# Inverting the triangular blocks of the last two chunks separately instead of as a pair

## The chip, the cores and the metric

The kernel runs on one core of a Trainium2 chip. The metric is the device time of one execution in microseconds (us); lower is better. A core has engines that run side by side, each with its own queue of instructions taken strictly in order: PE (TensorE: matrix products; PEld is its weight load), DVE (VectorE), ACT (ScalarE), POOL (GpSimd) and SP (SyncE, which here only issues transfers). An instruction whose inputs are not there holds up everything behind it on its own engine.

## The reference

Two parts follow each other: a linear recurrence over time ("attention"), and a mixture of experts.

```python
for t in range(S):                      # S = 768 steps, 4 batches x 8 heads, D = 40
    y[:, :, t] = einsum('bhd,bhde->bhe', r_t, state)
    Sa = einsum('bhde,bhe->bhd', state, a_t)
    state = state * w_t[:, :, None, :] - Sa (x) b_t + v_t (x) k_t
...
P = exp(x @ w_gate - max)               # x = y as 3072 tokens x 320
for _ in range(8):
    P /= P.sum(1) + 1e-9; P /= P.sum(0) + 1e-9; P *= N / E
out = sum over 8 experts of P[:, e:e+1] * (relu(x @ w1[e]) @ w2[e])
```

## The kernel before

The 768 time steps are cut into 12 **chunks** of 64, and the recurrence is rewritten so that within a chunk everything is a matrix product, except that a unit triangular 64x64 matrix has to be inverted for each chunk, batch and head. One chunk of one batch (four pairs of heads) is a **step**, written (chunk, batch). The order of the work comes from a table of events, each with a due time: `prep` (L112) reads the inputs of a step, forms products with running decays, and writes the triangular matrix to a scratch tensor `ld` in DRAM; `recur` (L262) runs the recurrence of a step in five stages, PE and DVE in turn: av (PE) - f (DVE L279) - xc (PE) - pu (PE L297) - pm (DVE L299) - c (PE) - ws (DVE L306) - y, z - zt (PE), then the same batch of the next chunk. Four batches are in flight, one stage apart. A scheduler then fixes each engine's instruction order from the table and its own cost model.

**The inversion** stands between prep and recurrence. The list `GROUPS` says which chunks are inverted together; `GRP` gives each chunk its group and place. A chunk has 4 batches x 8 heads = 32 matrices, each cut into two 32x32 diagonal blocks, so it fills 64 partitions, and a pair of chunks fills 128. One inversion of a group is: `load_lu` (L363) loads the blocks from DRAM into the tile `lu`; `flip_l` (L192, L193), `inv_diag` (L176, L179), `flip_d` (L196), `contract` (L185, L188), `flip_h` (L199) compute the inverse in the tiles `un` and `tn` with DVE instructions alone; `finish` (L358, L360, L361) makes a transposed copy and writes `un` and `tn` to the DRAM tensors `ud` and `nd`. There is one set of tiles `lu`, `un`, `tn`, `pr`, `gt` for all groups. `tload` (L225) loads a chunk's part of them back into the tiles `td`, `lg` and `tt`, and `tmat` (L246) makes the missing off-diagonal block with products gp (L253) and op (L258), twice per chunk, for batches 0-1 and 2-3. The products pu of the chunk (L297) need the result.

The due time of a group's inversion follows its last prep; that of the preps follows the number of the group's first chunk (`t0`).

**The expert part** starts while the recurrence ends: `prep_w` (L497) loads raw weights `ws` (L500) and splits them with ACT and POOL, `prep_x` (L530) reloads the tokens (`xs`, L535 and L537) and splits them with DVE (lines L544 to L560, three units of 128 columns for each of the four parts `s` of the tokens), and then PE runs 128 blocks of products p (L572) and op (L637). Its staging tiles lie where the tiles of prep and inversion lay, so the first load of `ws` comes behind the last inversion.

Of the kernel before, what the change touches and what calls it, by code (L numbers as in the profile page):

```python
# [28 lines left out]
def attention(ctx, tc, d, xd, ps, pq, pt, gs, lg):  # L29
# [355 lines left out]
    for c in range(NCH):  # L385
# [5 lines left out]
        for half in range(2):  # L391
            ev.append((t + 2 * SKEW * half, tmat, (c, half)))
    for s, cs in enumerate(GROUPS):
        us = slice(0, 64 * len(cs))
# [17 lines left out]
            pass  # L412


GROUPS = [[0, 1], [2, 3], [4, 5], [6, 7], [8, 9], [10, 11]]
GRP = {c: (i, j) for i, g in enumerate(GROUPS) for j, c in enumerate(g)}
P0 = -8
PD = 0.75
# [418 lines left out]
```

## Time and profile before

| | us |
|---|---|
| median of 3 runs | 1893.79 (1890.14 to 1895.72) |
| the profiled execution | 1882.69 |
| its span | 1880.9 |
| PE busy in the span | 1774.0 (94%) |
| DVE busy in the span | 1365.8 (73%) |
| the recurrence's last pm (L299) starts at | 548.2 |

The page cuts the span into 40 slices of 47 us; its first 12 slices are the recurrence, the rest are the experts. Rows of a group show the time busy and the mean of one instruction, then the idle time of the engine ahead of it with what ended that. The clock rows (PEclk) give the share of full clock that PE was granted: in this trace it is 1 or 0.5 at any moment, so a window's 0.74 is a mixture. A step (c, b) is known by counting pm, L299: there are 48 of them. PE durations overlap each other, so time is read from starts, or from windows.

### The profile page before, as it was taken

How to read it: one execution, taken by the hardware profiler on the slowest of the kernel's cores; microseconds unless marked ns; L12 is line 12 of the kernel's file. 1: busy time of each engine (PE TensorE's matmuls, PEld its weight loads, DVE VectorE, ACT ScalarE, POOL GpSimd, SP SyncE). 2: the span in 40 equal slices, each digit the busy share in tenths (PEclk: the TensorE clock that was granted, in tenths of full speed). 3: DMA queues.
4: the chain of work that ended last, by engine and by line, in shares of the span. 5: the costliest groups of instructions: out<-in, count | busy, mean ns of one | idle time of the engine just before them, and what ended most of it. 6: DMA issues, size and time to landing. Idle time of an engine off the chain costs nothing.

```text
span 1880.9 us, 31865 instructions
## 1 busy us (share of the span) xinstructions
PE 1774.0 (94%) x12035; PEld 1733.0 (92%) x12035; DVE 1365.8 (73%) x2378; ACT 854.6 (45%) x1845; POOL 867.8 (46%) x846
## 2 busy tenths in 40 slices
PE   4489998899898999999999999999999999999999
PEld 4378887899788899999999999999999999999999
DVE  7865867848558867776777767886776867777676
ACT  6356667466543434343443434445343433434342
POOL 6545546331444345281744628004471826537170
PEclk8579989789689999999999999999999999999999
DMA  7578776685621111020111102111110201111011
GB/s 192 114 152 175 149 174 158 120 140 109 168 67 46 37 37 55 20 74 18 57 37 37 56 19 74 55 33 37 37 55 19 73 19 55 37 37 59 16 37 43
DMA packets 187839, 136.27 MB, mean 72 GB/s; under 512 B 155941, under 2 KB 165285, under 8 KB 187685
## 3 DMA queue, kind: packets, MB, share of 16 engines
q1 hardware_dynamic: 184485, 128.98, 27.7%
q10 hardware_dynamic: 3200, 5.25, 1.1%
q8 instruction: 95, 1.56, 0.4%
q14 instruction: 59, 0.48, 0.1%
HBM read 113.74 MB, written 20.45 MB: 71 GB/s over the span
## 4 chain that ended last, share of the span: by engine, by line
PE 78%; DVE 7%; DMA 7%; POOL 3%; issue 2%; ACT 2%; SPq 1%; ACTq 0%; POOLq 0%; DVEq 0%
PE op L637 35%; PE p L572 32%; DMA inp<-in_inp_dram 3%; PE xc L286 2%; PE pu L297 1%; PE ll L151 1%; PE av L278 1%; PE c L304 1%; PE lp L334 1%; DMA nd<-tn 1%; PE gp L253 1%; DVE pr L185 1%; DMA rb<-in_r_dram 1%; PE op L258 1%; POOL ab L146 1%
## 5 line engine op out<-in xcount | busy, mean ns | idle before, releaser
L572 PE MATMUL p<-xch,wh 128*128 128x384 f32 (+1 forms) x1792 | 605.6, 339 | 6.9 <-DVE u L590 2.4
L593 ACT ACTIVATE hh<-sm 128x384 fp32r<-128x384 f32 x512 | 269.4, 526 | 722.9 <-DVE sm L590 722.9
L637 PE MATMUL op<-wh,hh 128*128 128x320 f32 x1536 | 477.8, 312 | 2.9 <-ACT hh L593 2.8
L637 PE MATMUL op<-wl,hh 128*128 128x320 f32 x1536 | 475.6, 310 | 0.0
L637 PE MATMUL op<-wh,hl 128*128 128x320 f32 x1536 | 468.8, 311 | 2.4 <-DVE hl L596 2.4
L518 POOL TENSOR_TENSOR wl<-ws,wh 128x640 fp32r<-128x640 f32 x60 | 103.3, 1721 | 608.7 <-ACT wh L516 608.5
L596 DVE SCALAR_TENSOR_TENSOR hl<-sm,hh 128x384 fp32r<-128x384 f32 x512 | 368.0, 752 | 2.2 <-ACT hh L593 2.0
L572 PEld LDWEIGHTS p<-xch,wh 128*128 128x128 f32 (+1 forms) x1792 | 337.8, 189 | 10.4 <-DVE u L590 4.1
L572 PE MATMUL p<-xcl,wh 128*128 128x384 f32 x896 | 302.9, 338 | 0.0
L572 PE MATMUL p<-xch,wl 128*128 128x384 f32 x896 | 302.3, 337 | 0.0
L637 PEld LDWEIGHTS op<-wh,hh 128*128 128x128 f32 x1536 | 291.1, 189 | 3.7 <-ACT hh L593 3.7
L637 PEld LDWEIGHTS op<-wl,hh 128*128 128x128 f32 x1536 | 291.6, 190 | 0.0
L637 PEld LDWEIGHTS op<-wh,hl 128*128 128x128 f32 x1536 | 287.6, 188 | 3.2 <-DVE hl L596 3.1
L590 DVE TENSOR_TENSOR sm<-p,u 128x384 f32<-128x384 f32 x384 | 234.8, 621 | 8.8
L572 PEld LDWEIGHTS p<-xcl,wh 128*128 128x128 f32 x896 | 168.9, 188 | 0.0
L572 PEld LDWEIGHTS p<-xch,wl 128*128 128x128 f32 x896 | 168.8, 188 | 0.0
L590 DVE TENSOR_TENSOR sm<-p,p 128x384 f32<-128x384 f32 x128 | 71.3, 557 | 129.7 <-PE p L572 76.9
L590 DVE TENSOR_TENSOR p<-p,p 128x384 f32<-128x384 f32 x128 | 71.2, 556 | 103.6 <-PE p L572 101.6
L590 DVE TENSOR_TENSOR u<-p,p 128x384 f32<-128x384 f32 x128 | 70.8, 553 | 59.8 <-PE p L572 58.7
L526 POOL TENSOR_TENSOR wl<-ss,wh 128x512 fp32r<-128x512 f32 x60 | 90.8, 1514 | 35.3 <-ACT wh L523 31.2
L151 PE MATMUL ll<-ab,kb 104*128 104x128 f32 x336 | 63.7, 349 | 45.9 <-POOL ab L146 21.8
L151 PEld LDWEIGHTS ll<-ab,kb 104*128 104x128 f32 x336 | 55.5, 250 | 50.7 <-POOL ab L146 30.2
(166 smaller groups left out, 2793.9 us busy)
## 6 DMA issues: line engine op xcount, KB each, us to landing
ws<-in_wts_dram SPq DMA_DIRECT2D x60, 832.0 KB
inp<-in_inp_dram SPq DMA_DIRECT2D x42, 521.6 KB
rb<-in_r_dram SPq DMA_DIRECT2D x48, 208.0 KB
ld<-lt ACTq DMA_DIRECT2D x40, 128.0 KB
vz<-in_v_dram SPq DMA_DIRECT2D x48, 104.0 KB
f<-in_vt_dram SPq DMA_DIRECT2D x48, 80.0 KB
xd<-y SPq DMA_DIRECT2D x96, 40.0 KB
st<-in_inp_dram SPq DMA_DIRECT2D x6, 521.6 KB
```

Source lines behind the costliest of these rows:

```text
L146: eng.tensor_tensor(out=ab[64:104, :, 64:128], in0=a_in[64:104], in1=g[64:104], op=ALU.mult)
L151: nc.tensor.matmul(ll[:, p], lhsT=kb[:, p], rhs=ab[:, p], start=True, stop=True)
L185: nc.vector.tensor_tensor(out=prv, in0=a.unsqueeze(2).broadcast_to([nu, n_c, n_r, n_k]), in1=m.unsqueeze(1).broadcast_to([nu, n_c, n_r, n_ ...
L253: nc.tensor.matmul(gp[:, p], lhsT=lb[:, p], rhs=t1[:, p], start=True, stop=True)
L286: nc.tensor.matmul(xc[h][:, p], lhsT=pp["sx"][:, p, h], rhs=f[:, p, h], start=True, stop=True)
L518: g.tensor_tensor(out=wl[:, 0:640], in0=raw[:, 256:896], in1=wh[:, 0:640], op=ALU.subtract)
L526: g.tensor_tensor(out=lv[:, 3:7], in0=so[:, :, 0], in1=hv[:, 3:7, 0], op=ALU.subtract)
L572: nc.tensor.matmul(o, lhsT=w_, rhs=x_, start=(j == 0), stop=(j == 3))
L590: eng.tensor_tensor(out=out, in0=x, in1=y, op=ALU.add)
L593: nc.scalar.activation(out=hh[:, f, h], in_=sm[f][:, h], func=AF.Relu)
L596: v.scalar_tensor_tensor(out=hl[:, f, h], in0=sm[f][:, h], scalar=0.0, in1=hh[:, f, h], op0=ALU.max, op1=ALU.subtract)
L637: nc.tensor.matmul(ops[i], lhsT=a[:, h, cs], rhs=w_[:, cw], start=(f == 0 and h == 0 and j == 0), stop=(last and h == 1 and j == 2))
```

## The change

The pair [10, 11] becomes two groups. Nothing else in the text changes; each of the two groups now has its own scratch tensors, loads, inversion, and write-back.

```diff
-GROUPS = [[0, 1], [2, 3], [4, 5], [6, 7], [8, 9], [10, 11]]
+GROUPS = [[0, 1], [2, 3], [4, 5], [6, 7], [8, 9], [10], [11]]
 GRP = {c: (i, j) for i, g in enumerate(GROUPS) for j, c in enumerate(g)}
```

What it does to the table of events: the inversion of chunk 10 is due right behind the four preps of chunk 10, and that of chunk 11 behind those of chunk 11, where both were due behind all eight. The first prep of chunk 11 is due 0.69 of a time unit later (five units are a chunk), the other seven as before. Two inversions of 64 partitions stand where one of 128 stood.

On DVE, before: the paired inversion starts behind ws of step (8,0) (L192, L193 first), and pm of step (8,1) is its first neighbour.

```order
L299 TENSOR_TENSOR pm<-pu,cst 128x416
L339 COPY lg<-lp 64x8
L279 TENSOR_TENSOR f<-av,cst 104x8x64
L306 TENSOR_TENSOR ws<-c_4497,c_202 104x416
L192 COPY lu<-lu 128x2x8x8
L193 COPY lu<-lu 128x16x16
L176 TENSOR_TENSOR pr<-un,lu 128x4
L299 TENSOR_TENSOR pm<-pu,cst 128x416
```

On DVE now, at the place where the inversion of chunk 10 begins; the pm in this piece is that of step (7,1), and L128 and L120 belong to preps of chunk 11.

```order
L161 TENSOR_TENSOR st_186<-ll,cst 64x8x64
L128 SCALAR_TENSOR_TENSOR st_187<-inp,g_196 104x256
L192 COPY lu<-lu 64x2x8x8
L193 COPY lu<-lu 64x16x16
L176 TENSOR_TENSOR pr<-un,lu 64x4
L299 TENSOR_TENSOR pm<-pu,cst 128x416
L179 TENSOR_REDUCE un<-pr 64x4
L176 TENSOR_TENSOR pr<-un,lu 64x16
L179 TENSOR_REDUCE un<-pr 64x4x2
L120 SCALAR_TENSOR_TENSOR q<-inp,cst 104x260
```

It begins four steps earlier than the pair did. It ends (L358) between pm of (8,2) and pm of (8,3); the inversion of chunk 11 follows at once and ends behind pm of (10,1), where the pair's ended behind pm of (9,3). DVE has 39 instructions more, one inversion.

On PE, before: between pu of (9,3) (first row) and pu of (10,0) (last row) stand the products gp and op of chunk 10's first half, directly behind each other.

```order
L297 MATMUL pu<-x_4892,tt_191 128x104 x4
L286 MATMUL xc_4969<-f,sx_173 104x104 x4
L286 MATMUL xc_4970<-f,sx_173 104x104 x4
L278 MATMUL av<-rb,vz_198 104x128 x4
L324 MATMUL zt<-cst,z 40x104 x4
L304 MATMUL c_5010<-pm,bb_170 104x104 x4
L253 MATMUL gp<-td,lg 64x32 x8
L258 MATMUL op<-td,lg 64x32 x8
L334 MATMUL lp<-gs,y 64x8 x4
L297 MATMUL pu<-x_4985,tt_190 128x104 x4
```

On PE now, one chunk later: from pu of (10,2) to pu of (10,3), with gp of chunk 11's first half. Chunk 10's own gp stands behind pu of (9,2) and its op behind pu of (9,3).

```order
L297 MATMUL pu<-x_5171,tt_190 128x104 x4
L286 MATMUL xc_5216<-f,st_185 104x104 x4
L286 MATMUL xc_5217<-f,st_185 104x104 x4
L278 MATMUL av<-rb,vz_201 104x128 x4
L324 MATMUL zt<-cst,z 40x104 x4
L253 MATMUL gp<-td,lg 64x32 x8
L304 MATMUL c_5289<-pm,bb_182 104x104 x4
L297 MATMUL pu<-x_5232,tt_190 128x104 x4
```

What moved: gp of the last inverted chunk has a whole step of other products between it and the inversion's end, where it had less than one.

On SP now, where the first weights of the expert part are loaded (ws, L500); f in the first row is that of step (11,2), before it was that of (10,3) which stood nearest ahead of them.

```order
L267 DMA rb<-in_r_dram 104x512 x2
L269 DMA f<-in_vt_dram 64x8x40
L500 DMA ws<-in_wts_dram 128x1664 x2
L535 DMA xs<-xd 128x2x256
L312 DMA xd<-y 40x4x64 x2
L537 DMA xs<-xd 32x2x256 x3
```

These loads stand three steps further back in the recurrence than before, and so do the DVE instructions of prep_x (L544 to L560): the first of them stood between pm of (10,0) and pm of (10,1), now it stands behind pm of (11,0). The order of the blocks from the thirteenth on is unchanged.

## The prediction

> **What bounds the kernel now.** I read the page's slices first, then windows around the recurrence's end, then the chain of waits there.
>
> ```profile
> PE   4489998899898999999999999999999999999999
> PEclk8579989789689999999999999999999999999999
> ```
>
> From slice 13 on PE is full at full clock, so the experts run at PE's rate and the change can only move the moment from which they do. The windows (columns: stretch, length, then busy time and instruction count of PE, PEld, DVE, ACT, POOL, then granted clock, DMA share, GB/s) show how PE gets there.
>
> ```profile
> 390.00:428.00 38.00, 38.00 (x331) 34.98 (x329) 14.04 (x26) 24.48 (x62) 13.28 (x19) 0.87 0.76 121
> 428.00:468.00 40.00, 40.00 (x407) 37.63 (x406) 36.58 (x68) 24.29 (x62) 6.74 (x9) 1.00 0.46 100
> 468.00:473.00 5.00, 0.53 (x6) 0.38 (x5) 1.00 (x3) 1.79 (x6) 0.00 (x0) 0.89 0.86 209
> 473.00:491.00 18.00, 17.17 (x108) 15.73 (x109) 2.81 (x8) 4.73 (x12) 3.53 (x5) 0.50 0.86 215
> 491.00:527.00 36.00, 32.48 (x228) 29.42 (x228) 25.16 (x39) 22.95 (x49) 26.96 (x26) 0.70 0.54 143
> 468.00:553.00 85.00, 76.17 (x570) 69.59 (x569) 38.01 (x71) 38.96 (x88) 34.20 (x35) 0.74 0.48 123
> 553.00:582.00 29.00, 22.59 (x113) 20.83 (x112) 26.37 (x35) 15.08 (x27) 24.96 (x22) 0.82 0.32 98
> ```
>
> Up to 468 PE is never idle, even from 428 on, where the paired inversion fills DVE (36.58 of 40.00). At 468 it stops for almost 5 us, and then works 18 us at half clock. The chain of waits (start, length, what) names the cause.
>
> ```profile
> 464.05 1.16 DVE un L188
> ...
> 466.14 0.62 DVE tn L358
> ...
> 466.79 3.42 DMA nd<-tn
> ...
> 470.62 2.17 DMA td<-nd
> 472.79 0.14 issue
> 472.92 1.90 PE gp L253 x16
> ```
>
> The inversion of chunks 10 and 11 is late by one round trip through DRAM: its last contraction ends at 465.2, `tn` is written back and reloaded, and gp of chunk 10 starts at 472.92. PE waits for nothing longer between 465 and 553 (waiter, awaited, total, times, longest):
>
> ```profile
> PE gp L253 <- DMA td<-nd: 4.5, 1, 4.5
> PE zt L324 <- DVE pm L299: 2.1, 1, 2.1
> ...
> PE op L258 <- ACT lg L255: 0.8, 1, 0.8
> ```
>
> The cost of this stall: 4.5 + 0.8 us idle, and 18.00 us at clock 0.50, which are 9 us lost; together 14.3 us.
>
> **The change, part by part.**
>
> *The second inversion on DVE.* One inversion, from the groups of DVE lines between 428 and 467 (count, busy us, mean ns, idle):
>
> ```profile
> L185 DVE TENSOR_TENSOR pr<-un,lu 128x1024 f32<-128x1024 f32 (+1 forms) x5 | 5.3, 1054 | 0.0
> L185 DVE TENSOR_TENSOR pr<-gt,tn 128x1024 f32<-128x1024 f32 (+1 forms) x5 | 5.1, 1019 | 0.0
> L188 DVE TENSOR_REDUCE un<-pr 128x64 f32<-128x512 f32 (+2 forms) x5 | 5.0, 998 | 0.1
> L188 DVE TENSOR_REDUCE gt<-pr 128x64 f32<-128x512 f32 (+2 forms) x5 | 5.0, 992 | 0.0
> ...
> L176 DVE TENSOR_TENSOR pr<-un,lu 128x4 f32<-128x4 f32 (+6 forms) x7 | 2.1, 295 | 0.2
> L179 DVE TENSOR_REDUCE un<-pr 128x4 f32<-128x4 f32 (+6 forms) x7 | 1.7, 237 | 0.1
> ```
>
> These are 24.2 us; five copies of some 0.4 us (the rest of the 39 instructions) make it 26. Does half the partitions make them shorter? Two rows of equal free size but 64 and 104 partitions (start, length):
>
> ```profile
> 399.58 0.68 DVE L161 TENSOR_TENSOR st<-ll,cst 64x512 f32<-64x512 f32 x1 [2.32 <-PE ll L151]
> 407.06 0.69 DVE L279 TENSOR_TENSOR f<-av,cst 104x512 f32<-104x512 f32 x1 [0.89 <-PE av L278]
> ```
>
> They do not differ, so DVE gets 26 us of new work. It lies between pm of (7,1) and pm of (8,3), that is from about 390 to 440. Up to 428 DVE was idle for 38.00 - 14.04 = 24 us. I walked its new order against the old starts: at no ws, f or pm is it behind PE by more than some 2 us before it has caught up, and the most inversion work between two pm is 6.5 us (two steps (9,0) to (9,2) bore as much with PE full). Behind that, the inversion of chunk 11 is spread over seven steps like the pair's was, in the region that had no PE idle. So the cover holds; without it the price is between 0 and 26 us. One place can break it: the first copy (L192) waits for `lu` from DRAM and holds DVE meanwhile. I take 2 us for this part.
>
> *The stall at chunk 10.* Its inversion now ends some seven steps ahead of its pu, so the 14.3 us go.
>
> *What is late next: the inversion of chunk 11.* Its L358 stands behind pm of (10,1). From the end of pu(10,1), pm, z and L358 take 1.4 us; from L358's end the chain above took 472.92 - 466.76 = 6.2 us to gp; that is 7.6. PE's order has ahead of that gp two xc, one op, two av, two zt, one c, one pu and some lp, about a step and a half, and a step is 40.00 / 6 = 6.7 us in the window from 428: about 10 us. So 2 us of slack, and I take no stall; the price if it is gone is the same 14.3.
>
> *The recurrence's end.* Of the 570 PE instructions from 468 to 553, 25 are the experts' (rows of p, L572, and of the experts' op, L637):
>
> ```profile
> 468.00:553.00 85.00, 5.66 (x22) 3.93 (x23) 0.74 0.48 123
> ...
> 468.00:553.00 85.00, 0.60 (x3) 0.51 (x3) 0.74 0.48 123
> ```
>
> The other 545, at 40.00 / 407 = 0.098 us each, are 53.6 us: unstalled, the recurrence leaves PE at 468 + 53.6 = 521.6 instead of 553.
>
> *The start of the experts.* Here the change takes back. The weights' loads now stand behind the vt-load of (11,2), which waits until xc of (10,3) has freed its buffer: three steps behind pu(10,0), or 468 + 3 x 6.7 = 488, where it was
>
> ```profile
> 478.97 0.53 SPq L500 DMA_DIRECT2D ws<-in_wts_dram  x1
> ...
> 489.75 0.43 DVE L544 TENSOR_TENSOR xt<-xs 128x256 f32<-128x256 f32 x1 [1.79 <-DMA f<-in_vt_dram]
> ...
> 518.64 1.11 DVE L560 TENSOR_TENSOR xch<-xt,xch 32x512 fp32r<-32x512 f32 x1
> ```
>
> From there to the first DVE instruction of prep_x took 10.8 us, from that to the last 30.0. The same gives 498.8 and 528.8; with DVE never idle (25.16 busy of 36 in 491 to 527) the second could be 25. I take 525 for the third product, the first to need all three units. PE, done at 521.6 + 2, then waits a little, and I charge 7 of the 9 us of half clock for it (0 to 9). Eight product instructions stand ahead of that point. Now compare the moments at which the experts, had they run without pause, would have begun. Before: 25 instructions, 6.26 us at clock 0.74, are 4.6 us of work done by 553, so 548.4. After: 525 + 7 - 8/25 x 4.6 = 530.5. Gain 17.9.
>
> The Trainium skill's "TensorE: Matmul & The Clock Gate", Part 1, says that the clock halves after an idle window of about 3.4 us. The stall of 4.5 us above agrees; a wait as short as the one expected here would by that rule cost no clock, and the sum would be 7 us better. The trace is less kind: from 491 to 527, with no single wait over 2.1 us, the clock was 0.70.
>
> *POOL behind the recurrence.* Before, POOL had also prepared part of the third and fourth weights and of the next tokens by 527:
>
> ```profile
> 518.00 1.20 POOL L510 TENSOR_TENSOR ss<-ws 128x256 f32<-128x256 f32 x1
> ...
> 526.87 0.71 POOL L549 TENSOR_TENSOR xt<-xs,xt 128x256 f32<-128x256 f32 x1
> ```
>
> Eight such instructions, some 7 us, now fall into the transition, where POOL was busy 24.96 of 29.00 us. The third weights are first needed two blocks after the start, so most is hidden: 0 to 7, I take 2.
>
> **Sum.** 17.9 - 2 - 2 = 13.9, 14 us gained: 1882.7 - 14 = 1868.7 on the profiled execution's time, which is 11.1 us below the median shown, and 1893.8 - 14 = **1880 us** on the median.
>
> **Rivals.**
>
> *DVE becomes the bound where chunk 10 is inverted* (slower). The place is the first copy and the seven steps behind it; it decides once the wait for `lu` holds DVE longer than its slack. For it speaks chunk 6, where this happened:
>
> ```profile
> 316.66 0.56 DVE L299 TENSOR_TENSOR pm<-pu,cst 128x416 f32<-128x416 f32 x1
> ...
> 328.95 1.91 SPq L369 DMA_DIRECT2D lu<-ld  x4
> ...
> 336.52 0.27 DVE L192 COPY lu<-lu 128x128 f32<-128x128 f32 x1 [2.48 <-DMA f<-in_vt_dram]
> ...
> 374.55 0.58 DVE L299 TENSOR_TENSOR pm<-pu,cst 128x416 f32<-128x416 f32 x1
> ...
> 412.92 0.56 DVE L299 TENSOR_TENSOR pm<-pu,cst 128x416 f32<-128x416 f32 x1
> ```
>
> `lu` came 5.7 us after its last issue, and chunk 6 took 57.9 us where chunk 7, without an inversion, took 38.4. Against it: chunk 6 also had the DRAM round trip, and its inversion stood denser. If all 26 us land on the path: 1880 + 24 = 1904. The Trainium skill's "Trainium Kernel Development and Optimization", Best Practices, says always to tile to 128 partitions; by that rule this rival is the expected case, and the two rows of 64 and 104 partitions agree that a half-empty instruction costs as much. Chance 0.15.
>
> *The stall only moves to chunk 11.* For it: the slack is 2 us, and chunk 11's write-back shares SP with other loads. It costs 14.3 and leaves 1894: no change. Chance 0.14.
>
> *The preparation of the experts is the bound.* It decides if the chain from the first ws to the dense products, 548.4 - 479.0 = 69.4 us, does not shrink: 488 + 69.4 = 557.4, 9 us later than before, 1903. Against it: much of those 69 us was DVE and ACT waiting in order for a PE at half clock. Chance 0.10.
>
> *The change doesn't do what it says*: a transfer or a shared tile could keep chunk 10's inversion from ending early. The orders show it ended before (8,3), so I give this no chance of its own.
>
> **How the numbers follow.** The forecast, 1865 to 1888 by its own bounds (no lost clock and no POOL cost at the lower end, x0 at 528.8 and twice the other costs at the upper), has 0.57; 0.04 is left for anything else, half of it below. About 0.3% (6 us) is what a measurement can tell from no change. Faster than 1888: 0.60. Within: most of the moved stall and a part of the others, 0.18. Slower than 1899.5: the first and third rival's greater part, 0.22. The range leaves out the far end of both slow rivals and a little below: 1864 to 1900.
>
> **What would show it.** Right: no PE wait of gp for td from 440 to 530, two L192 about 40 us apart, the last pm at about 517 instead of 548, the first ws load near 488, DVE 26 us busier. Wrong: gp of chunk 11 waiting for td (moved stall); pm steps of (7,1) to (8,3) longer than before's (DVE); the last pm early but the dense products not before 550 (preparation). Were the round trip not the cause of the half clock at 473, the largest term would fall.

## The result and the profile after

| | before | after |
|---|---|---|
| median of the timing (us) | 1895.28 (20 executions, 1883.07 to 1915.49) | 1886.16 (20 executions, 1874.41 to 1905.31) |
| ratio, 95% interval | | 0.9935 [0.9909, 0.9961] |
| profiled execution, its span (us) | 1882.69, 1880.9 | 1879.67, 1877.9 |
| DVE busy (us) | 1365.8 | 1390.9 |
| start of pm of (6,3), (9,3), (11,3) (us) | 374.5, 465.6, 548.2 | 381.5, 477.5, 543.4 |

The change makes the kernel 0.65% faster. A second timing, reported below, gave 0.9969 [0.9938, 1.0001], so the gain is some 6 to 12 us, and its size is known less well than its sign. Single executions more than 1.5% above the fastest of their kernel are left out of every ratio here.

The first two parts of the page after, instructions by engine and two rows of the 40 slices, show one more inversion on DVE (25.1 us more) and PE full from one slice earlier on than before.

```profile
PE 1769.5 (94%) x12035; PEld 1728.3 (92%) x12035; DVE 1390.9 (74%) x2417; ACT 855.3 (46%) x1845; POOL 867.5 (46%) x846
...
PE   4478988899979999999999999999999999999999
...
PEclk8579989689969999999999999999999999999999
```

The same windows as the prediction's, cut at pm of (6,3), (9,3) and (11,3) of the changed kernel (columns: stretch, length, busy time and count of PE, PEld, DVE, ACT, POOL, then granted clock, DMA share, GB/s):

```profile
381.50:477.50 96.00, 93.67 (x843) 86.40 (x841) 72.08 (x139) 58.25 (x147) 29.25 (x38) 0.89 0.64 125
477.50:500.00 22.50, 22.50 (x226) 20.67 (x225) 15.56 (x27) 13.03 (x34) 3.96 (x4) 1.00 0.49 102
500.00:530.00 30.00, 25.93 (x240) 23.83 (x239) 19.24 (x28) 20.82 (x44) 17.44 (x17) 0.85 0.62 182
530.00:543.40 13.40, 13.40 (x79) 12.69 (x79) 7.06 (x15) 4.28 (x8) 6.00 (x6) 0.57 0.37 111
```

Where PE stood and then crawled at half clock (468 to 491 before) there are now 22.5 us without a gap at clock 1.00. But the last 13.4 us of the recurrence run at 0.57, and from 500 on 4 us are idle. The stretch from pm of (9,3) to pm of (11,3) as a whole, before and after:

```profile
465.60:548.20 82.60, 73.78 (x557) 67.43 (x555) 36.65 (x67) 40.02 (x90) 34.00 (x35) 0.73 0.52 131
477.50:543.40 65.90, 61.83 (x541) 57.19 (x539) 41.86 (x69) 38.13 (x85) 27.41 (x27) 0.84 0.52 140
```

The waits of PE from 440 to 553 in the trace after (waiter, awaited, total, times, longest) are complete here, and no gp waits for td among them:

```profile
PE xc L286 <- DVE ws L306: 2.3, 1, 2.3
PE xc L286 <- DVE f L279: 1.7, 1, 1.7
PE p L572 <- ACT p L599: 1.3, 1, 1.3
PE p L572 <- DVE xch L560: 0.5, 1, 0.5
PE c L304 <- DVE pm L299: 0.5, 1, 0.5
PE p L572 <- DVE xcl L558: 0.3, 1, 0.3
```

What waits is now held up by DVE, but for one wait of 1.3 us for ACT. The views of single lines (median duration, first and last start) place the two inversions, the pm from (6,3) to (11,3), and the first loads of weights:

```profile
L192 DVE COPY lu<-lu x2: 257/260/264, 400.6 to 439.6; 64x128 f32<-64x128 f32 x2
...
  DMA lu<-ld: 6.9, 2
...
L358 DVE COPY tn<-un x2: 366/368/369, 448.7 to 492.6; 64x256 f32<-64x256 f32 x2
...
L299 DVE TENSOR_TENSOR pm<-pu,cst x21: 553/576/592, 381.5 to 543.4; 128x416 f32<-128x416 f32 x21
...
L500 SPq DMA_DIRECT2D ws<-in_wts_dram x3: 419/698/1661, 502.6 to 515.2; - x3
```

The row behind L192 says that DVE sat idle 6.9 us for the loads of `lu`, 4.3 and 2.6 for the two inversions; for the pair it had been 2.1 before. The first of these waits is the place that the prediction named as the weak one: pm of (7,1) stands right behind it, and the step from pm of (7,0) to it takes 14.0 us, before it was 6.8 (in the second traces, below, 12.5 and 7.1). PE shows no wait for it, and how much of the longer step is due to it is not separated. Chunk 10's inversion ends at 448.7, which is 29 us ahead of pm of (9,3). The difference of the two profiled executions can be split by these marks. Up to pm of (6,3) nothing is changed in the order, yet the trace after is 7.0 us later there. That is the scatter of executions: the kernel before, in its second trace, gets there at 380.9, the changed kernel at 381.8. From (6,3) to (9,3) it loses 4.9 us (91.1 to 96.0), from (9,3) to (11,3) it wins 16.7 (82.6 to 65.9), from there to the thousandth matmul of the experts it loses 2.0 (184.0 to 186.0), and the rest is equal within 0.3. The sum is -3 us, the difference of the spans; without the first 7.0 it is -10, in line with the timing.

### The profile page after: what moved, and what is told of

Its sections match the earlier page's. It is cut to its first block, busy times and chain, and to the rows that moved or that the text cites. A ratio compares the mean times of both kernels' runs of the same rounds, so it can differ in the third digit from the quotient of the medians.

```text
span 1877.9 us, 31907 instructions
## 1 busy us (share of the span) xinstructions
PE 1769.5 (94%) x12035; PEld 1728.3 (92%) x12035; DVE 1390.9 (74%) x2417; ACT 855.3 (46%) x1845; POOL 867.5 (46%) x846
## 4 chain that ended last, share of the span: by engine, by line
PE 76%; DVE 3%; DMA 1%; issue 0%; ACT 0%; SPq 0%; POOL 0%; DVEq 0%; POOLq 0%; ACTq 0%
PE op L637 35%; PE p L572 33%; PE xc L286 2%; PE av L278 1%; PE pu L297 1%; PE lp L334 1%; PE c L304 1%; DMA xs<-xd 1%; DVE hl L596 1%; DVE sm L590 1%; PE op L258 0%; PE ll L151 0%; PE zt L324 0%; PE gp L253 0%; DMA inp<-in_inp_dram 0%
## 5 line engine op out<-in xcount | busy, mean ns | idle before, releaser
L572 PEld LDWEIGHTS p<-xch,wh 128*128 128x128 f32 (+1 forms) x1792 | 338.0, 189 | 10.5 <-DVE u L590 2.8
L590 DVE TENSOR_TENSOR p<-p,p 128x384 f32<-128x384 f32 x128 | 71.1, 555 | 102.0 <-PE p L572 100.6
## 6 DMA issues: line engine op xcount, KB each, us to landing
inp<-in_inp_dram SPq DMA_DIRECT2D x42, 521.6 KB
st<-in_inp_dram SPq DMA_DIRECT2D x6, 521.6 KB
```

Source lines behind the costliest of these rows:

```text
L572: nc.tensor.matmul(o, lhsT=w_, rhs=x_, start=(j == 0), stop=(j == 3))
L590: eng.tensor_tensor(out=out, in0=x, in1=y, op=ALU.add)
```

## The experiments

Each ratio is against the kernel before timed beside it on the same chip, with its 95% interval. Three chips were used: one for the new DVE work alone, the first run with the stall alone removed, the earlier loads and the further split; one for the two kernels again, the odd pairs and the first run with both edits; one for the rest. The stretch from pm of (9,3) to pm of (11,3) is the measure in the traces; a row shown for a run is that stretch.

### The two kernels again

No edit. The question was whether the two traces that the prediction and the comparison rest on are typical.

> The kernel before once more, for a second trace. Its profiled execution (1882.7 us) is at the low end of its runs (1883 to 1918, median 1898), and removing the stall alone brought 27.7 us where the prediction read 14.3 from that trace. Theory A (that trace shows a mild case of the stall): a second trace shows a longer wait of gp for td at chunk 10 or more half clock behind it, and pm of (9,3) to pm of (11,3) takes 88 to 100 us instead of 82.5. Theory B (the stall is as read, and the rest of the 27.7 us lies elsewhere): 80 to 85 us again. The ratio is 1.000 in both.

> The changed kernel once more, beside the others on one chip and for a second trace. Ratio 0.991 to 0.996 as before. If the change is stall-free in general, pm of (9,3) to pm of (11,3) takes 62 to 69 us again and no gp waits for td from 440 us on; if chunk 11's slack of some 2 us is used up in some executions, one of its gp products waits for td and the stretch takes 75 us or more.

Measured: before 1896.22 us, ratio 1.0006 [0.9974, 1.0037]; after 1889.57 us, ratio 0.9969 [0.9938, 1.0001]. The kernel before again, its stretch and PE's longest wait between 440 and 553:

```profile
471.70:557.50 85.80, 78.22 (x555) 71.00 (x554) 38.04 (x66) 40.17 (x90) 33.79 (x35) 0.70 0.50 126
```

```profile
PE gp L253 <- DMA td<-nd: 4.7, 1, 4.7
```

The changed kernel again:

```profile
478.70:551.60 72.90, 70.41 (x542) 65.15 (x540) 41.99 (x69) 38.22 (x85) 27.14 (x27) 0.74 0.48 127
```

The stall of before is as it was read (4.7 us of wait after 4.5; 85.8 us after 82.6), so theory A falls. The changed kernel has no wait of gp for td here either, but its stretch took 72.9 us instead of 65.9, above the 62 to 69 us expected of a stall-free execution and below the 75 expected with a stall: PE was idle only 2.5 us, and the clock was 0.74 where it had been 0.84. Cut at pm of (10,3), the two parts are:

```profile
478.70:513.30 34.60, 34.60 (x274) 32.02 (x273) 17.23 (x31) 15.76 (x40) 4.25 (x5) 0.75 0.45 93
513.30:551.60 38.30, 35.81 (x271) 33.13 (x269) 24.76 (x40) 22.46 (x45) 22.89 (x23) 0.73 0.50 157
```

In the first part PE is never idle in the records and still has a clock of 0.75; in the first trace this part took 26.7 us at 1.00. So the stretch varies by its clock, without any one wait. The whole time does the same: of twelve executions the fastest took 1878.6 us at a mean clock of 0.949, the slowest 1902.2 at 0.935.

### The new DVE work alone

The kernel before, with an additional inversion of chunk 10, due right behind its preps, whose results go to scratch tensors of its own (`start_x`) that nothing reads.

```diff
         ev.append((t + INV_DT * 10 + 0.01, finish, (s, us)))
+        if cs == [10, 11]:
+            tx = 35.23
+            ux = slice(0, 64)
+            ev.append((tx, start_x, ()))
+            ev.append((tx, load_lu, ("x", 1)))
+            for i, (fn, a) in enumerate(INV):
+                ev.append((tx + INV_DT * 10 * i / len(INV), fn, (ux,) + a))
+            ev.append((tx + INV_DT * 10 + 0.01, finish, ("x", ux)))
```

> The kernel before, with a further inversion of chunk 10 alone on 64 partitions behind the preps of chunk 10, whose results go to two scratch tensors that nothing reads; the pair (10,11) is inverted as before and used. It adds the change's work on DVE, and nothing else of it: the wait for the round trip at chunk 10 and the start of the experts stay. Prediction's theory (the new DVE work is hidden but for some us; the two traces differ by 4.9 us from pm of (6,3) to pm of (9,3)): 2 to 5 us slower than before, ratio 1.001 to 1.003. Rival (DVE is the bound where chunk 10 is inverted): all 26 us are on the path, ratio 1.013. Under both, PE still waits 4 to 5 us for td at chunk 10.

Measured: 1903.02 us, ratio 1.0032 [1.0004, 1.0061], 6 us slower (1 to 12). Its waits of PE from 480 to 512:

```profile
PE gp L253 <- DMA td<-ud: 16.4, 1, 16.4
```

The ratio lies at the upper end of what the prediction's theory expected, but the wait of 4 to 5 us that both expectations shared is not there, so this is not the clean price that was wanted. The new work pushed the pair's inversion back (its L358 starts 10.5 us behind pm of (9,3), before it was 0.5), and the wait for the round trip grew from 4.5 to 16.4 us. What it shows is weaker, and still against the prediction: the 26 us do not vanish in DVE's idle time, since here the work queued behind them ends ten us later.

### The stall alone

The kernel before; chunk 10 takes its inverse from chunk 8's tensors, so nothing waits for the write-back.

```diff
         ld, ud, nd = invs[GRP[c][0]]
+        if c == 10:
+            ud, nd = invs[4][1:]
```

> The kernel before, but chunk 10 takes its td and tt from the inverse of chunk 8, which is in DRAM long before, so that nothing waits for the write-back of the pair (10,11) at chunk 10; the inversion itself runs as before. The output then isn't the reference's. Left out is the wait alone, with no more work on DVE and the weights' loads where they were. Prediction's theory (the round trip costs 4.5 + 0.8 us of idle PE and 9 us of half clock, and the start of the experts is not put off): 14 to 25 us faster, ratio 0.987 to 0.993, pm of (9,3) to pm of (11,3) in 54 to 68 us instead of 82.6. Rival (the preparation of the experts is the bound, so an earlier end of the recurrence is worth little): last pm earlier, but the hundredth matmul of the experts at most 5 us earlier, ratio 0.997 to 1.000. Rival (the half clock has another cause than the wait): 4.5 to 5.3 us faster, the clock from gp of chunk 10 on still at 0.5, ratio 0.997.

> The kernel before with chunk 10 fed from the inverse of chunk 8, once more, on one chip with the three runs beside it. If removing the stall is worth what the first run of it showed: 0.981 to 0.990 against before. If that run was an outlier of its eight executions: 0.990 to 0.996, as the changed kernel.

Measured: 1872.50 us, ratio 0.9854 [0.9813, 0.9895], and in a second timing on another chip 1874.84 us, 0.9881 [0.9843, 0.9920]. The mean is 0.987, 25 us. The stretch in the two runs, first and second:

```profile
484.80:548.50 63.70, 62.63 (x544) 58.09 (x544) 38.83 (x66) 39.22 (x87) 32.76 (x33) 0.84 0.60 159
```

```profile
470.70:532.20 61.50, 57.13 (x544) 52.84 (x544) 39.32 (x66) 39.26 (x87) 31.93 (x33) 0.92 0.63 165
```

Without the stall the stretch takes 62.6 us instead of 84.2 (means of two traces each), 21.6 less. This splits by the clock records: before, 44.4 and 51.8 us of it were at half clock, here 20.5 and 10.2, which is 16.4 us of lost work, and idle time was 8.8 and 7.6 us, here 1.1 and 4.4, another 5.4. The theory that most of the half clock comes with the wait holds, and both rivals fall. One reservation: the scheduler also moved the experts' first loads here, by two steps of the recurrence (46 vt-loads ahead of them instead of 44; the changed kernel has 47), so the 25 us are the stall with that move. The second trace, cut at pm of (10,3):

```profile
470.70:498.80 28.10, 27.46 (x275) 25.11 (x276) 10.02 (x22) 16.56 (x40) 7.37 (x9) 1.00 0.79 194
498.80:532.20 33.40, 29.67 (x271) 27.73 (x269) 29.30 (x45) 22.70 (x48) 24.56 (x24) 0.85 0.49 140
```

### Stall removed and new DVE work together

Both edits above at once. The orders of DVE and PE around chunks 7 to 10 are then nearly the changed kernel's, and the weights' loads stand one vt-load further back than it has them (48 ahead of them), two further than with the stall alone removed.

> The kernel before with both additions at once: the further inversion of chunk 10 that nothing reads, and chunk 10 fed from the inverse of chunk 8. Its orders of DVE and PE around chunks 7 to 10 are nearly those of the changed kernel, but nothing can wait at chunk 10; against the run with chunk 10 fed from chunk 8 alone (0.9854) it adds only the 39 DVE instructions and what they push back. If the extra DVE work is what took the gain back: ratio 0.991 to 0.996, as the changed kernel. If the extra DVE work is hidden: 0.984 to 0.988, and the difference to the changed kernel lies in chunk 11's own inversion and write-back.

> Both additions again (stall removed, further inversion of chunk 10 that nothing reads), beside the run with the stall removed alone. If the new DVE work with what it pushes back is what takes the gain back, 0.992 to 0.998 here and at least 0.005 above the run without it; if the two runs differ by less than 0.003, the new DVE work is hidden, as the prediction had it.

Measured: 1887.73 us, 0.9954 [0.9919, 0.9989], and on the chip of the second run with the stall alone removed 1890.78 us, 0.9940 [0.9908, 0.9972]. That is the changed kernel's result, and 0.0100 and 0.0059 above the runs without the DVE work, 15 us in the mean (the intervals allow about 8 to 22). The first of these differences is between two chips; the second, on one chip, is 11 us (2 to 21). The stretch in the two runs:

```profile
474.90:539.50 64.60, 54.91 (x549) 51.57 (x547) 45.60 (x70) 38.41 (x86) 28.82 (x29) 0.95 0.56 152
```

```profile
481.40:564.70 83.30, 74.65 (x550) 69.57 (x548) 46.68 (x70) 38.40 (x86) 29.36 (x29) 0.69 0.46 118
```

The wait of PE that both have, here as the second shows it (481 to 565), is for DVE's copies of the gate's products (L339 of the kernel before):

```profile
PE lp L336 <- DVE lg L341: 7.0, 3, 5.0
```

These copies do not stand behind the added inversion, which had ended at 447.0 and 453.0. They stand behind the preparation of the tokens, here in the first execution, where PE's wait ends at 523.8:

```profile
518.13 3.80 DVE L565 TENSOR_TENSOR xcl<-xs,xch 128x384 fp32r<-128x384 f32 x1
521.94 1.51 DVE L568 TENSOR_TENSOR xch<-xs,xch 32x384 fp32r<-32x384 f32 x1
523.49 0.16 DVE L341 COPY lg<-lp 64x8 f32<-64x8 f32 x1
```

PE was idle 9.7 and 8.7 us in the stretch, longer than in any stall-free run without the DVE work, and in the second execution 51 us fell at half clock, although no transfer was waited for. Of the two expectations the first holds: the new DVE work, with what it pushes back, is what takes the gain back. But what it pushes back includes the preparation: its first DVE instruction stands between pm of (11,0) and (11,1), with the stall alone removed it stands right behind pm of (10,3). The 15 us are the work with this shift.

### Which of it: the DVE work, or the late start of the experts

Two kernels on the changed one, in both of which the DVE instructions of chunk 11's inversion are left out and chunk 11 takes chunk 10's inverse. DVE then has as much to do as before. In the first, the tiles of the inversion come free early, so the weights' loads stand seven steps earlier than in the changed kernel (40 vt-loads ahead instead of 47); in the second a small copy holds the tiles until pm of (10,3), so that they stand at 47 again.

```diff
-        for i, (fn, a) in enumerate(INV):
+        for i, (fn, a) in enumerate(INV if cs != [11] else INV[:0]):
```

```diff
+        if (c, b) == (10, 3):
+            for t in (luf,):
+                nc.vector.tensor_copy(out=t[0:64, 0:1], in_=pm[0:64, 0, 0:1])
```

> The changed kernel without the DVE instructions of chunk 11's inversion, so chunk 11 takes the inverse of chunk 10 (the loads and the write-back of chunk 11 stay). No stall at chunk 10, no more DVE work than before, and the loads of the first weights seven steps earlier than in the changed kernel. If new DVE work and late start together take the gain back: 0.980 to 0.988. If neither does: 0.991 to 0.996, as the changed kernel. If DVE is the bound (rival 1 of the prediction): up to 24 us faster than the changed kernel.

> As the run beside it (the changed kernel without the DVE instructions of chunk 11's inversion), but a one-element copy from pm of (10,3) into the inversion's tile lu holds the tiles until there, so that the loads of the first weights stand as late as in the changed kernel. The difference to the run beside it is the late start of the experts alone; the difference to the changed kernel is the new DVE work alone. If the late start is what took the gain back (the prediction's working charged it 13 of 31 us): 8 us or more slower than the run beside it, ratio 0.988 to 0.995. If the DVE work did: within 4 us of the run beside it, 0.981 to 0.988.

Measured: early start 1889.72 us, 0.9960 [0.9928, 0.9992]; late start 1879.46 us, 0.9888 [0.9838, 0.9939]. Neither pair of expectations came as written. The early start's ratio is that of "neither does", and the late start's lies in the range given for a late start that costs 8 us or more; but the late start is not dearer than the early one, it is cheaper, by 0.0072 (about 0.001 to 0.013 from the two intervals). The stretch, with the early and then with the late start:

```profile
477.30:557.60 80.30, 78.52 (x543) 71.94 (x542) 33.38 (x60) 39.68 (x89) 29.28 (x31) 0.65 0.35 84
...
490.50:518.20 27.70, 25.92 (x167) 23.59 (x166) 19.42 (x30) 19.42 (x40) 18.98 (x17) 0.56 0.53 143
528.00:558.00 30.00, 30.00 (x195) 27.72 (x194) 6.30 (x14) 9.02 (x20) 2.19 (x3) 0.61 0.05 11
```

```profile
482.30:543.50 61.20, 58.44 (x552) 53.83 (x550) 31.54 (x60) 38.64 (x86) 23.85 (x25) 0.92 0.51 125
...
497.10:510.30 13.20, 13.20 (x139) 12.34 (x139) 4.55 (x12) 7.88 (x20) 1.78 (x3) 1.00 0.43 88
510.30:543.50 33.20, 30.44 (x279) 27.64 (x277) 22.47 (x40) 22.88 (x46) 20.30 (x21) 0.90 0.58 157
```

With the early start the preparation of weights and tokens falls between (10,1) and (10,3), where DVE is busy 19.42 of 27.70 us, and PE goes to clock 0.56 and stays low to the end. With the late start the same steps run at 1.00, and the preparation follows at the end, where the clock is 0.90 although DVE is as busy there (22.47 of 33.20 us). So a busy DVE alone does not explain the 0.56, and why the early place is dearer is not shown. A part of its price is seen ahead of the stretch: gp of chunk 10 starts at 468.3 after a wait of 2.4 us for a transfer, and the DMA share is 1.11 from 459 to 466, behind the loads of weights issued at 454.4 and 456.8. In the traces the early start won 7.7 us behind the last pm (180.4 against 188.1 us to the thousandth matmul) and lost 19.1 ahead of it. The late start with no new DVE work stands at 0.9888, level with the run with the stall alone removed on that chip (0.9881); the changed kernel, with its two timings' mean 0.9952, is 0.0064 above it, 12 us. So the late start took nothing measurable back, and the second inversion on DVE did. The interval of this last difference is wide (about 2 to 22 us), and it is between chips, but with the 15 us of the section above it points the same way. As there, the edit moves more than the work: the first DVE instruction of prep_x stands right behind pm of (11,0) in the changed kernel, here behind the f that follows, and the first xcl (L552) stands ahead of pm of (11,1) there, here behind it. What the busy time alone costs, and what the shift of the preparation, no run separates.

### Loading the experts' weights earlier

The changed kernel, with the pool of the inversion's tiles opened behind those of the prep, so that the experts' staging tiles do not lie under them.

```diff
-    inv = ctx.enter_context(tc.tile_pool(name="a_inv", bufs=1))
     sets = [ctx.enter_context(tc.tile_pool(name=f"a_set{i}", bufs=1)) for i in range(NSX)]
+    inv = ctx.enter_context(tc.tile_pool(name="a_inv", bufs=1))
```

> The changed kernel, with the inversion's tiles allocated behind the prep's sets, so that the staging tiles of the experts no longer lie under the inversion's: the first two loads of weights and the first unit of tokens stand some nine steps earlier on their queues, the other two units at (11,0) and (11,1). Prediction's theory (the late start of the experts takes gain back): the hundredth matmul of the experts 5 to 10 us earlier than in the changed kernel, so ratio 0.988 to 0.991 against before where the change alone had 0.9935. Rival (the experts' start is not what took the gain back, or early preparation disturbs DVE by as much as it brings): 0.993 to 0.995.

Measured: 1886.19 us, 0.9945 [0.9917, 0.9973]. The rival holds: the first weights are loaded at 450.3 instead of 502.6, and nothing comes of it. The hundredth matmul of the experts follows the last pm by 34.4 us, in the changed kernel by 30.3.

### A further pair split

```diff
-GROUPS = [[0, 1], [2, 3], [4, 5], [6, 7], [8, 9], [10], [11]]
+GROUPS = [[0, 1], [2, 3], [4, 5], [6], [7], [8, 9], [10], [11]]
```

> The changed kernel, with the pair (6,7) split as well. In the kernel before, chunk 6 waits for the loads of its blocks and for the round trip (step (6,0) takes 20.4 us, chunk 6 takes 57.9 us where chunk 7 takes 38.4). Theory (a split pays where the pair's inversion ends late, whatever the chunk): pm of (5,3) to pm of (6,3) shorter by 10 to 15 us, DVE's further 26 us cost 2 to 5, so 5 to 13 us faster than the changed kernel, ratio 0.987 to 0.991. Rival (here DVE is the bound, since preps and two inversions stand in chunks 4 to 7 together): 5 to 15 us slower than the changed kernel, ratio 0.996 to 1.002.

Measured: 1889.80 us, 0.9964 [0.9927, 1.0001], no better than the changed kernel and inside the range of the rival, DVE as the bound. The stretches of chunk 6, chunk 7, the first half of chunk 8 and what follows up to pm of (9,3), and then the waits of PE from 409 to 445:

```profile
337.30:376.90 39.60, 37.90 (x362) 34.27 (x361) 33.02 (x66) 26.23 (x68) 22.93 (x27) 1.00 0.85 170
376.90:409.50 32.60, 29.36 (x263) 26.78 (x262) 29.58 (x48) 22.54 (x57) 20.17 (x21) 0.95 0.66 137
409.50:443.10 33.60, 27.87 (x189) 25.59 (x188) 28.11 (x48) 14.73 (x38) 6.99 (x11) 0.63 0.62 111
443.10:494.20 51.10, 51.10 (x415) 47.06 (x414) 38.16 (x67) 22.99 (x59) 5.95 (x9) 0.78 0.39 82
```

```profile
PE gp L253 <- DMA td<-nd: 3.3, 1, 3.3
```

The split does for chunk 6 what it does for chunk 10: 39.6 us where it was 57.9, at clock 1.00. But the two inversions fill DVE (29.58 of 32.60 us in chunk 7) and push that of the pair (8,9) back, and now chunk 8 waits: (8,0) and (8,1) take 33.6 us. From pm of (6,3) to (9,3) it takes 117.3 us, 21 more than in the changed kernel. So the rival's reason holds in part: DVE is nearly full. What neither expectation had is how it costs: the stall went to the next pair.

### The odd pairs

```diff
-GROUPS = [[0, 1], [2, 3], [4, 5], [6, 7], [8, 9], [10], [11]]
+GROUPS = [[0], [1, 2], [3, 4], [5, 6], [7, 8], [9, 10], [11]]
```

> Chunk 0 and chunk 11 are inverted alone and the others in the pairs (1,2), (3,4), (5,6), (7,8), (9,10): as many instructions on DVE as the changed kernel has. Every pair is as close to its use as before, but the first inversion needs four preps, not eight. Theory (a pair's inversion ends late wherever the recurrence runs at PE's rate, so the stall of chunk 10 goes to chunk 9): a gp of chunk 9 waits for td by 2 us or more, and the stretch from pm of (8,3) to pm of (11,3) is no shorter than in the kernel before; with a first pm 5 to 15 us earlier, ratio 0.990 to 1.000. Rival (the last group alone is what matters): no such wait, ratio 0.984 to 0.990.

Measured: 1889.34 us, 0.9965 [0.9932, 0.9998]. Waits of PE from 440 to 500:

```profile
PE gp L253 <- DMA td<-nd: 6.4, 1, 6.4
```

The theory holds: gp of chunk 9 now waits 6.4 us, pm of (8,3) to pm of (11,3) takes 116.1 us against 107.4 before, and the first pm comes at 109.8 us against 114.1 (119.0 in the second trace of before). So chunk 10 was not special as a chunk; the wait goes with the first chunk of a pair.

## Why the prediction was right, and where its terms were not

The time, 1886, lies 6 us above the forecast of 1880 and inside the range; faster was the likeliest case. That it came so near is in part luck: three terms were wrong, and their errors largely cancelled. The end of the recurrence was put some 11 us too early by its rate, the new DVE work 10 to 13 us too cheap, and the start of the experts some 11 us too dear.

- *The second inversion on DVE, 2 us, "so the cover holds".* This step failed. With the stall gone, the new DVE work cost 15 us by the pair of runs that differ by it, 12 by the changed kernel against its version without chunk 11's inversion; both with the preparation shifted. The traces place it from (9,3) to (11,3), with 71.7 us in the mean of the four with the extra work and the stall gone against 62.6 in the two with the stall alone removed, and they show two parts. From pm of (10,3) on, where the added work is already done, all four take longer: 38.3 to 42.4 us (the changed kernel with earlier loads takes 38.0) against 33.2 to 34.4 (late start included), with the preparation in another place. Ahead of it two of the four keep to 26 or 27 us, and two take 34.6 and 40.9, with 17 and 34 us at half clock and no idle time of PE; without the extra work it is 28 to 29 (41 with the early start). From (6,3) to (9,3) the sign that the prediction gave for DVE is there, 96.0 and 96.9 us against 91.1 and 90.8, but the traces with the old order of DVE go up to 96.6, and the late start, which has no more DVE work than before, takes 96.2. The walk through the order asked whether DVE falls behind PE. What it left out is the shift of the preparation, and that PE can lose clock without a wait on record: in the changed kernel's second trace the stretch was 72.9 us long with only 2.5 us of idle PE. That the new work causes the half clock is likely from these counts and not shown. The upper bound of 26 was kept for the range, and the value lies between the ends.
- *The stall at chunk 10, 14.3 us.* The mechanism was right: no gp waits for td in either trace of the changed kernel. The size was right for the stretch it was read from, but the half clock that follows reaches further than the 18 us counted; over the whole stretch 21.6 us went with the stall. The sum did not use the 14.3 but the end of the recurrence, below.
- *What is late next, chunk 11, no stall.* Right in both traces. A slack of 2 us was enough here, though the two runs with other groups show how easily a stall moves to another pair.
- *The recurrence leaves PE at 521.6.* Wrong by its rate. The 0.098 us for an instruction came from a window at clock 1.00. Free of the stall, the stretch needed 61.2 to 63.7 us in three runs without extra DVE work (80.3 with the early start), with 10 to 20 us of them at half clock, where the prediction's last pm at 517 means 51. The last pm came at 543.4; 12 us of that is the shift that was there by pm of (9,3), and 7 of these 12 the scatter ahead of (6,3).
- *The start of the experts.* The prediction let the experts begin 0.2 us behind the last pm before (548.4 against 548.2), and 13.5 behind it now (530.5 against 517): 13 us taken back. The mean way from the last pm to the thousandth matmul grew from 184.4 to 186.8 us, so it is 2 to 3 us, and the run with the late start shows no loss from it in the whole time. The first load of weights came 25 us behind pm of (9,3) in one trace and 32 in the other, against 22 predicted; but the recurrence ended later than thought and covered the preparation, which left the steps of chunk 10 alone.
- *POOL behind the recurrence, 2 us.* Not separated from the term above; it is within those 2 to 3 us.
- *Rivals.* DVE as the bound was right in kind and half right in size: 12 to 15 of its 24 us, though mostly not at the place it named, the steps (7,1) to (8,3). The moved stall did not appear in the changed kernel. The preparation as the bound did not either: its condition was that the way from the first ws load to the experts does not shrink, and to their hundredth matmul that took 71.1 us after (502.6 to 573.7) and 96.2 before (479.0 to 575.2).
- *The clock.* The Trainium skill's "TensorE: Matmul & The Clock Gate", Part 1, puts the half clock behind an idle window of about 3.4 us and gave a sum 7 us better. The runs agree on the unit: of the 227 half-clock stretches in the fourteen traces 213 last a multiple of 3.41 us, all but one in each trace. They do not bear out that a shorter wait costs no clock: the changed kernel's longest wait from 440 on was 2.3 us, and its clock was 0.57 from 530 to 543. Leaving that gain out of the sum was right.

What stays open: which small gaps cost a window of half clock and which don't. The kernel with both edits had 6.8 us of half clock in the stretch in one execution and 51 in another, and no wait in the traces tells the two apart. Open as well is how the 12 to 15 us divide between the new DVE work itself and the shifted preparation.

None of the runs that keep the whole computation beats the changed kernel. The runs without new DVE work, but for the one with the early start, stand at 0.985 to 0.989 and show what a way to end the pair's inversion earlier without a second one would be worth.

## What to carry to other kernels

Work that fits an engine's idle time need not be free when the bounding engine works with that engine step by step: price it from a run that has the extra work and nothing else of the change, look at what else its order moves, and look at the granted clock of the stretch as well as at the waits. A stall behind a batch goes when the batch is cut, but check what is queued behind it, since in both other groupings tried here another pair stalled instead. Preparing the next phase as early as its buffers allow can cost more than it brings, as the early start of the experts did here.

## What the runs showed of the hardware

- Half clock without a wait: in the run with the early start PE was busy 30.00 of 30.00 us from 528 to 558 and had a granted clock of 0.61. The waits before it, from 484 on, were 1.2 and 0.6 us.
- Clock lost with no idle time on record: from pm of (9,3) to pm of (10,3) PE is busy throughout in both traces of the changed kernel, by records in which the ends of products are modelled: 26.70 us at clock 1.00 in one and 34.60 at 0.75 in the other, with 272 and 274 matrix products.
- The scatter of this kernel goes with the clock. Over the ten timings here that keep eleven or more executions, the correlation of time with mean clock lies between -0.85 and -0.96. In the early start's, the slowest of eleven took 1897.6 us at 0.936 and the fastest 1873.4 at 0.950; time and clock multiplied give 1776 and 1780. A single trace is therefore a sample of some 1% of scatter, and the stretch in question has to be compared between marks of its own, not by spans.
